# First DFT block turned by TensorE, columns taken in fours, and mod's shift row summed by TensorE, in an FNet and gMLP block

## The chip, the cores and the metric

The kernel runs on one core of a Trainium2 chip. A core has five engines, each with an instruction queue of its own that runs in order: TensorE (matrix products, PE in the profile, with its weight loads as PEld), VectorE (DVE), ScalarE (ACT), GpSimd (POOL) and SyncE (SP, which here only issues DMA transfers). The metric is the time on the device in microseconds, the median of several runs.

## What is computed

```python
mod = (_silu(c) @ w_mod).reshape(c.shape[0], 6, 1, -1)
sa, ca, ga, sb, cb, gb = (mod[:, 0], mod[:, 1], mod[:, 2], mod[:, 3], mod[:, 4], mod[:, 5])
h = _layernorm(x, axis=-1) * (1 + ca) + sa
x = x + ga * _A_ref(h, A_dft_seq_re, A_dft_seq_im, A_dft_hid_re, A_dft_hid_im)
h = _layernorm(x, axis=-1) * (1 + cb) + sb
x = x + gb * _B_ref(h, B_w_in, B_w_sp, B_b_sp, B_w_out)
```

`x` has 2048 rows of 512 floats. `_A_ref` is a Fourier mixing: h is multiplied by two 512 x 512 matrices along the columns and by two 2048 x 2048 matrices along the rows, `y = Cr a - Ci b` with `a = h Hr^T`, `b = h Hi^T`. `_B_ref` is a gated MLP: `z = gelu(h w_in)`, its second half is normed and multiplied by the 2048 x 2048 matrix `w_sp` along the rows, the result gates the first half, and `w_out` brings it back to 512 columns.

## The kernel before

**Products.** Each factor is split into a high part of reduced precision (fp32r) and the rest, its low part; a product a b is the sum of three (high high, high low, low high), issued by `matmul3` at L79, L80 and L81. The 2048 x 2048 matrices are read from memory in blocks of 512 x 512 and cut into chunks of 128 of their columns: a chunk n must stand with its column index on the partitions, that is transposed, and 512 row indices along the row.

**Main loop.** `src` lists the blocks: first those of Cr and Ci for the row quarter t = 0 (for each quarter g of the columns one of Cr, one of Ci), then t = 1 to 3, then h2 from memory, then w_sp. `load` brings block b into one of two buffers `stage`, as four transfers of 32 partitions (`load_block`, L131), in an order from which VectorE's transpose of 32 x 32 squares (`squares`, L142) makes chunk k. `prep_hi` (L153) makes T (transposed, by VectorE) and the high part ah (ScalarE, L165), `prep_lo` the low part al (VectorE, L174). `prep(n)` runs ahead: high part of chunk n + 3, low part of n + 2. `mm_a(n)` issues the twelve products of chunk n into four PSUM banks `gp`: four column groups k of h, three products each. Behind it `run(n)` issues what the table `fill` holds for this place (`at(n, f, ...)`), in the order in which it was entered. The order on each engine is the order in which the program issues (a manual schedule).

**Rows of x.** There are sixteen row tiles s of 128 rows. `load_x(g)` brings four; `stats_x` takes mean and variance (VectorE L87, L89), GpSimd makes the factor from them (L91, L92, L99), `norm_x` applies them on ScalarE (L103), `scale_x` multiplies by 1 + ca (L278), `shift_x` adds sa (L281). `hi_h` (ScalarE, L296) and `lo_h` (VectorE, L301) split the result into hh and hl. Tile 3 goes through `make_x` on VectorE (L287, L288). From tile 4 on, scaling and shift run on GpSimd. Chunk n of t = 0 multiplies tile s = 4 (n div 8) + n mod 4, so tiles 0 to 3 serve chunks 0 to 7, and tile 4 is first needed by chunk 8.

**mod.** The rows ca (number 1) and sa (number 0) are wanted at the start. Row 1 is summed by TensorE: four products of w_mod with a spread silu(c) (`scb`), in plain fp32 (L227). Of row 0, three quarters are summed by VectorE (L215, L220) and one by TensorE, which then spreads the sum over the partitions with a product by ones (L229). `keep_mod` copies the sum to SBUF (ScalarE, L209). `keep_busy` multiplies ones without use of the result (L236).

**Start.** SyncE issues x (tiles 0 to 2), w_mod for rows 1 and 0, block 0, x (tile 3), block 1 and x (tiles 4 to 7).

Of the kernel before, what the change touches and what calls it, by code (L numbers as in the profile page):

```python
# [8 lines left out]
F32 = mybir.dt.float32  # L9
# [4 lines left out]
P = 128  # L14
# [5 lines left out]
def fnet_gmlp_kernel(  # L20
# [115 lines left out]
    def load(b):  # L136
        if b < len(src):
            stage[b] = blocks.tile([P, 16, P], F32, tag="stage", bufs=2, name=f"stage{b}")
            load_block(stage[b], src[b])

    def squares(dst, block, k):
        nc.vector.transpose(dst.rearrange("p (b i) -> p b i", i=32), block[:, :, 32 * k:32 * k + 32])  # L142

    prepared = set()

    def prep(n):

        if n not in prepared:
            prepared.add(n)
            prep_hi(n + 3)  # L150
            prep_lo(n + 2)

    def prep_hi(n):  # L153
        if n >= NE:
            return
        b, k = divmod(n, 4)
        T[n] = blocks.tile([P, Q], F32, tag="t", bufs=2, name=f"t{n}")
        if N3 <= n < N4:

            nc.vector.transpose(T[n].rearrange("p (k a i) -> p a k i", k=4, i=32),  # L160
                                stage[b][:, :, 32 * k:32 * k + 32].rearrange("p (a k) i -> p a k i", k=4))
        else:
            squares(T[n], stage[b], k)
        AH[n] = blocks.tile([P, Q], F32R, tag="ah", bufs=4, name=f"ah{n}")
        nc.scalar.activation(AH[n], T[n], AF.Copy)  # L165
        if k == 3:
            stage.pop(b)
            load(b + 2)

    def prep_lo(n):  # L170
        if n >= NE:
            return
        AL[n] = blocks.tile([P, Q], F32R, tag="al", bufs=3, name=f"al{n}")
        nc.vector.tensor_tensor(AL[n], T.pop(n), AH[n].bitcast(F32), op=ALU.subtract)  # L174


    p2 = ctx.enter_context(ExitStack())
# [9 lines left out]
    nc.scalar.dma_start(ccol, c.rearrange("b (k p) -> p (b k)", p=P))  # L187
    ones = cpool.tile([P, P], F32, name="ones")
    nc.gpsimd.memset(ones, 1.0)
    mhalf = cpool.tile([P, 1], F32, name="mhalf")  # L190
    nc.gpsimd.memset(mhalf, -0.5)
    sc = cpool.tile([P, ND], F32, name="sc")
# [8 lines left out]
    def load_mod(j):  # L201
        wm[j] = [SP[-1].tile([P, D], F32, tag=f"wm{k}", bufs=2 if len(SP) == 1 else 1, name=f"wm{j}_{k}") for k in range(ND)]
        for k in range(ND):
            nc.sync.dma_start(wm[j][k], w_mod[k * P:(k + 1) * P, j * D:(j + 1) * D])

    def keep_mod(j, ps, pl, plus_one):
        if j not in mods:
            mods[j] = pl.tile([P, D], F32, name=f"mod{j}")
        nc.scalar.activation(mods[j], ps, AF.Copy, bias=1.0 if plus_one else 0.0)  # L209
# [12 lines left out]
    def sum_mod_first(j, k, pl, plus_one, summed=0):  # L222

        ps = bank(k, f"modp{j}")
        w = wm.pop(j)
        for m in range(summed, ND):
            nc.tensor.matmul(ps, scb[:, m, :], w[m], start=m == summed, stop=not summed and m == ND - 1)  # L227
        if summed:
            nc.tensor.matmul(ps, ones, w[0], start=False, stop=True)  # L229
        keep_mod(j, ps, pl, plus_one)  # L230

    def keep_busy(n, k):
# [26 lines left out]
    def load_x(g, ks=range(4)):  # L259

        if g not in XG:
            XG[g] = spool.tile([P, 4, D], F32, tag="x", bufs=2, name=f"x{g}")
        k0, k1 = ks[0], ks[-1] + 1
        v = x.rearrange("(g a k i) d -> g a i k d", g=NQ, a=4, i=32)
        for a in range(4):
            nc.sync.dma_start(XG[g][32 * a:32 * a + 32, k0:k1, :], v[g, a][:, k0:k1, :])
        for k in ks:
            X[4 * g + k] = XG[g][:, k, :]

    def stats_x(s):  # L270
        NRM[s] = norm([X[s]], "x")

    def norm_x(s):
        LN[s] = spool.tile([P, D], F32, tag="xn", bufs=4, name=f"xn{s}")
        apply(LN[s], X.pop(s), NRM.pop(s))

    def scale_x(s, eng=nc.vector):
        eng.tensor_tensor(LN[s], LN[s], mods[1], op=ALU.mult)  # L278
# [10 lines left out]

    def parts_h(s, t):  # L290

        return t[s].rearrange("p k (a i) -> p k a i", i=32), LN[s].rearrange("p (a k i) -> p k a i", a=4, i=32)

    def hi_h(s):
        h_hi[s] = hpool.tile([P, ND, P], F32R, name=f"hh{s}")
# [17 lines left out]
    def mm_a(n):  # L313
        t, r = divmod(n, 8 * NQ)
        j, s = ((r // 4) % 2, r // 8 * 4 + r % 4) if t == 0 else (r // NS, r % NS)
        if s == 0:
            for k in range(ND):
                GP[t, j, k] = bank(4 * j + k if t == 0 else ring[0] % 6, f"gp{t}_{j}_{k}")
                ring[0] += t > 0
        ah, al = AH.pop(n), AL.pop(n)  # L320
        for k in range(ND):
# [62 lines left out]
    def load_wi(e, k0):  # L384

        raw = wpool[0].tile([P, 2, FH], F32, tag="wraw", bufs=2, name=f"wraw{e}_{k0}")
        v = w_in.rearrange("(a k i) f -> a i k f", a=4, i=32)
        for a in range(4):
            nc.sync.dma_start(raw[32 * a:32 * a + 32], v[a][:, k0:k0 + 2, e * FH:(e + 1) * FH])
        for k in range(2):  # L390
            wraw[e, k0 + k] = raw[:, k, :]

# [139 lines left out]
            mm([n])  # L532


    load_x(0, range(3))
    load_mod(1)
    load_mod(0)
    load(0)
    load_x(0, range(3, 4))
    load(1)  # L540
    load_x(1)
    keep_busy(2, 5)
    for s in range(3):
        stats_x(s)
    for s in range(3):
        norm_x(s)
    sum_mod(0, range(3))
    sum_mod_first(1, 7, spool, True)
    sum_mod_first(0, 6, spool, False, 3)
    keep_busy(3, 5)  # L550
    for s in range(3):
        scale_x(s)
    shift_x(0, nc.vector)
    hi_h(0)
    shift_x(1, nc.vector)
    hi_h(1)
    lo_h(0)
    shift_x(2, nc.vector)
    lo_h(1)
    prep_hi(0)  # L560
    prep_lo(0)
    hi_h(2)
    prep_hi(1)
    prep_lo(1)
    lo_h(2)
    make_x(3)
    prep_hi(2)
    at(0, hi_h, 3)
    at(1, lo_h, 3)
    at(1, load_x, 2)  # L570
    at(9, load_x, 3)
# [200 lines left out]
```

## Time and profile before

| | |
|---|---|
| median of 3 runs | 1002.78 us (1002.72 to 1003.27) |
| the profiled execution's own time | 1003.15 us |
| its span, first to last instruction | 1001.4 us |
| granted TensorE clock, mean | 0.997 |
| instructions | 11608 |
| moved by DMA | 114.28 MB |

The profile is one execution, taken by the hardware profiler. Busy time says how long an engine worked, not what the end waited for; a wait is put down to what came last before the engine went on. In a group of instructions the text reads out<-in, with partitions x elements, then the count, the busy time in us and the mean in ns, then the idle time of the engine just before them. L numbers are lines of the kernel before.

### The profile page before, as it was taken

The page shows a single profiled execution, that of the slowest core. Times are in us where ns is not written, and L with a number is a line of the kernel's source. Part 1 is how long each engine was busy: PE and PEld are TensorE (multiplying, and loading weights), DVE is VectorE, ACT ScalarE, POOL GpSimd, SP SyncE. Part 2 cuts the span into 40 slices and gives each one's busy share as a digit, 9 for nine tenths or more (in the row PEclk, how much of TensorE's full clock was granted, in tenths as well). Part 3 has the DMA queues.
Part 4 walks back from the last instruction along what each step waited for, and adds up shares of the span by engine and source line. Part 5 has one row for each costly group of instructions (what it writes and reads, how often), then busy time and mean ns, then how long its engine had stood idle before and what let it go on. Part 6 is the DMA issues. An engine that isn't in the chain of part 4 may idle for free.

```text
span 1001.4 us, 11608 instructions
## 1 busy us (share of the span) xinstructions
PE 988.9 (99%) x4350; PEld 818.5 (82%) x4350; DVE 543.1 (54%) x820; ACT 295.9 (30%) x450; POOL 172.9 (17%) x281
## 2 busy tenths in 40 slices
PE   7999999999999999999999999999999999999998
PEld 3878888788888888888888998888888888888886
DVE  6888864876475546547433676565332622262315
ACT  3444531332232313222543665431111111111101
POOL 1576002022210122004321121102000200020001
PEclk8999999999999999999999999999999999999999
DMA  9786761565355343555553132435225222532141
GB/s 250 150 189 138 157 147 53 137 168 137 95 138 114 83 119 98 123 126 163 190 204 116 43 80 48 116 68 152 65 63 158 53 64 64 158 67 50 42 137 43
DMA packets 145961, 114.28 MB, mean 114 GB/s; under 512 B 7024, under 2 KB 125808, under 8 KB 145904
## 3 DMA queue, kind: packets, MB, share of 16 engines
q1 hardware_dynamic: 139296, 93.61, 39.6%
q0 software_dynamic: 6080, 19.93, 5.4%
q8 instruction: 34, 0.56, 0.2%
q14 instruction: 23, 0.19, 0.1%
q10 hardware_dynamic: 528, 0.00, 0.0%
HBM read 93.59 MB, written 19.92 MB: 113 GB/s over the span
## 4 chain that ended last, share of the span: by engine, by line
PE 94%; POOL 2%; issue 1%; DVE 1%; DMA 1%; ACT 0%; SPq 0%; DVEq 0%; POOLq 0%
PE gp L81 11%; PE gp L80 11%; PE gp L79 10%; PE gw L79 10%; PE gw L81 10%; PE gw L80 10%; PE yp L81 3%; PE yp L80 3%; PE yp L79 3%; PE z2p L80 3%; PE z2p L79 3%; PE z2p L81 3%; PE z1p L79 3%; PE z1p L80 3%; PE z1p L81 3%; PE op L81 2%
## 5 line engine op out<-in xcount | busy, mean ns | idle before, releaser
L174 DVE TENSOR_TENSOR al<-t,ah 128x512 fp32r<-128x512 f32 x224 | 161.6, 721 | 271.6 <-PE gw L80 142.6
L165 ACT ACTIVATE ah<-t 128x512 fp32r<-128x512 f32 x224 | 141.8, 633 | 541.8 <-PE gw L81 212.2
L79 PE MATMUL gp<-ah,hh 128*128 128x512 f32 x512 | 201.1, 393 | 3.1 <-ACT ah L165 2.7
L80 PE MATMUL gp<-al,hh 128*128 128x512 f32 x512 | 200.7, 392 | 0.6 <-DVE al L174 0.6
L81 PE MATMUL gp<-ah,hl 128*128 128x512 f32 x512 | 200.4, 391 | 0.0
L81 PE MATMUL gw<-ah,zl 128*128 128x512 f32 x448 | 174.3, 389 | 0.0
L80 PE MATMUL gw<-al,zh 128*128 128x512 f32 x448 | 174.3, 389 | 0.0
L79 PE MATMUL gw<-ah,zh 128*128 128x512 f32 x448 | 174.3, 389 | 0.0
L142 DVE STREAM_TRANSPOSE t<-stage 128x512 f32<-128x512 f32 x208 | 146.2, 703 | 4.6 <-DMA stage<-in_A_dft_seq_im_dram 1.7
L79 PEld LDWEIGHTS gp<-ah,hh 128*128 128x128 f32 x512 | 96.8, 189 | 24.7 <-ACT ah L165 3.5
L80 PEld LDWEIGHTS gp<-al,hh 128*128 128x128 f32 x512 | 96.8, 189 | 21.9 <-DVE al L174 1.7
L81 PEld LDWEIGHTS gp<-ah,hl 128*128 128x128 f32 x512 | 96.8, 189 | 20.5 <-DVE hl L301 0.5
L81 PEld LDWEIGHTS gw<-ah,zl 128*128 128x128 f32 x448 | 84.1, 188 | 17.6
L80 PEld LDWEIGHTS gw<-al,zh 128*128 128x128 f32 x448 | 84.1, 188 | 17.4
L79 PEld LDWEIGHTS gw<-ah,zh 128*128 128x128 f32 x448 | 84.1, 188 | 17.3
L496 POOL TENSOR_TENSOR u<-u,g 128x512 f32<-128x512 f32 x16 | 21.4, 1339 | 336.1 <-DVE g L494 336.1
L367 POOL DMA_DIRECT2D x_d<-xr x16 | 8.8, 551 | 246.3 <-DVE xr L366 246.3
L79 PE MATMUL yp<-hth,gh 128*128 128x512 f32 x128 | 49.8, 389 | 0.0
L80 PE MATMUL yp<-htl,gh 128*128 128x512 f32 x128 | 49.8, 389 | 0.0
L81 PE MATMUL yp<-hth,gl 128*128 128x512 f32 x128 | 49.8, 389 | 0.0
L80 PE MATMUL z2p<-wil,ah 128*128 128x448 f32 x128 | 46.7, 365 | 0.0
L79 PE MATMUL z2p<-wih,ah 128*128 128x448 f32 x128 | 46.7, 365 | 0.0
(106 smaller groups left out, 1165.4 us busy)
## 6 DMA issues: line engine op xcount, KB each, us to landing
stage<-in_A_dft_seq_re_dram SPq DMA_DIRECT2D x64, 256.0 KB, 4.8
stage<-in_A_dft_seq_im_dram SPq DMA_DIRECT2D x64, 256.0 KB, 5.0
stage<-in_B_w_sp_dram SPq DMA_DIRECT2D x64, 256.0 KB, 4.7
stage<-h_d SPq DMA_DIRECT2D x32, 256.0 KB, 4.6
z_d<-z POOLq DMA_DIRECT2D x28, 256.0 KB, 5.6
u<-z_d SPq DMA_DIRECT2D x4, 1792.0 KB, 8.2
wm<-in_w_mod_dram SPq DMA_DIRECT2D x24, 256.0 KB, 5.5
xr<-in_A_x_dram POOLq DMA_DIRECT2D x16, 256.0 KB, 3.2
```

What stands on the lines that cost most here:

```text
L79: nc.tensor.matmul(acc, ah, bh, start=first, stop=False)
L80: nc.tensor.matmul(acc, ah, bl, start=False, stop=False)
L81: nc.tensor.matmul(acc, al, bh, start=False, stop=last)
L142: nc.vector.transpose(dst.rearrange("p (b i) -> p b i", i=32), block[:, :, 32 * k:32 * k + 32])
L165: nc.scalar.activation(AH[n], T[n], AF.Copy)
L174: nc.vector.tensor_tensor(AL[n], T.pop(n), AH[n].bitcast(F32), op=ALU.subtract)
L367: nc.gpsimd.dma_start(x2_d[t][i * P:(i + 1) * P, :], x2)
L496: eng.tensor_tensor(U[t][:, f, :], U[t][:, f, :], g, op=ALU.mult)
```

## The change

It has four parts.

- **Block 0** is loaded as whole rows (`load_whole`: four transfers of 128 partitions) and turned by TensorE: `turn(k)` issues four transposes of 128 x 128 against an identity into a PSUM bank, from which the high and the low part of chunk k are taken. The high part of chunk 0 is made by VectorE. The identity is made on GpSimd at the start.
- **Columns in fours.** Chunk k of a block is no longer made of four runs of 32 columns but of every fourth column, k, k + 4, k + 8 and so on. VectorE's transposes read their source in steps of four floats. The rows of x are tiled alike: tile k of a quarter holds every fourth row, so a partition's four rows lie side by side in memory; h is read in steps of four floats when it is split (`parts_h`), and w_in is loaded likewise. For the four chunks a quarter of the second GELU half, the step lies in the reading of T (`like`).
- **x by tile**: one transfer for each `load_x` in place of four, and at the start one for tiles 0 and 1, one for tile 2, one for tile 3.
- **mod's row 0** is summed by TensorE alone. Tile 0 gets its shift straight from PSUM. The idle products behind it are gone. Tile 3 is normed on ScalarE like the others.

The first chunk's twelve products are issued in another order: four by ah, four by al, four with hl.

```diff
+    def load_whole():
+        stage[0] = blocks.tile([P, 16, P], F32, tag="stage", bufs=2, name="stage0")
+        v = stage[0].rearrange("p (q a) s -> p q (a s)", q=4)
+        for q in range(4):
+            nc.sync.dma_start(v[:, q, :], src[0][128 * q:128 * q + 128, :])
+
+    def turn(k):
+        T[k] = bank(4 + k, f"t{k}")
+        v = stage[0].rearrange("p (q a) (i k) -> p q k (a i)", q=4, k=4)
+        for q in range(4):
+            nc.tensor.transpose(T[k][:, 128 * q:128 * q + 128], v[:, q, k], ident)
+
     def squares(dst, block, k):
-        nc.vector.transpose(dst.rearrange("p (b i) -> p b i", i=32), block[:, :, 32 * k:32 * k + 32])
+        nc.vector.transpose(dst.rearrange("p (b i) -> p b i", i=32),
+                            block.rearrange("p b (i k) -> p k b i", k=4)[:, k])
...
+    def like(a, n):
+        return a.rearrange("p (k m) -> p k m", k=4) if N3 <= n < N4 else a
...
-        T[n] = blocks.tile([P, Q], F32, tag="t", bufs=2, name=f"t{n}")
-        if N3 <= n < N4:
-            nc.vector.transpose(T[n].rearrange("p (k a i) -> p a k i", k=4, i=32),
-                                stage[b][:, :, 32 * k:32 * k + 32].rearrange("p (a k) i -> p a k i", k=4))
-        else:
+        if n > 3:
+            T[n] = blocks.tile([P, Q], F32, tag="t", bufs=2, name=f"t{n}")
             squares(T[n], stage[b], k)
         AH[n] = blocks.tile([P, Q], F32R, tag="ah", bufs=4, name=f"ah{n}")
-        nc.scalar.activation(AH[n], T[n], AF.Copy)
+        if N3 <= n < N4:
+            T[n] = T[n].rearrange("p (m k) -> p k m", k=4)
+        if n == 0:
+            nc.vector.tensor_copy(AH[n], T[n])
+        else:
+            nc.scalar.activation(like(AH[n], n), T[n], AF.Copy)
...
+    ident = spool.tile([P, P], F32, name="ident")
+    make_identity(nc, ident)
...
-        v = x.rearrange("(g a k i) d -> g a i k d", g=NQ, a=4, i=32)
-        for a in range(4):
-            nc.sync.dma_start(XG[g][32 * a:32 * a + 32, k0:k1, :], v[g, a][:, k0:k1, :])
+        v = x.rearrange("(g p k) d -> g p k d", g=NQ, k=4)
+        nc.sync.dma_start(XG[g][:, k0:k1, :], v[g][:, k0:k1, :])
...
-        return t[s].rearrange("p k (a i) -> p k a i", i=32), LN[s].rearrange("p (a k i) -> p k a i", a=4, i=32)
+        return t[s], LN[s].rearrange("p (m k) -> p k m", k=4)
...
-    load_x(0, range(3))
+    load_x(0, (0, 1))
     load_mod(1)
+    load_x(0, (2,))
     load_mod(0)
-    load(0)
-    load_x(0, range(3, 4))
+    load_whole()
+    load_x(0, (3,))
     load(1)
     load_x(1)
     keep_busy(2, 5)
...
-    sum_mod(0, range(3))
     sum_mod_first(1, 7, spool, True)
-    sum_mod_first(0, 6, spool, False, 3)
-    keep_busy(3, 5)
...
+    ps = sum_mod_first(0, 6, spool, False)
+    turn(0)
+    turn(1)
+    nc.vector.tensor_tensor(LN[0], LN[0], ps, op=ALU.add)
     hi_h(0)
+    prep_hi(0)
+    prep_lo(0)
+    prep_hi(1)
+    lo_h(0)
     shift_x(1, nc.vector)
     hi_h(1)
+    prep_lo(1)
     lo_h(1)
...
+    prepared.add(0)
+    at(0, turn, 2)
+    at(0, turn, 3)
+    at(0, prep_hi, 2)
+    at(0, stats_x, 3)
+    at(0, norm_x, 3)
+    at(0, shift_x, 2, nc.vector)
+    at(0, hi_h, 2)
+    at(0, prep_lo, 2)
+    at(0, lo_h, 2)
+    at(0, prep_hi, 3)
+    at(0, scale_x, 3)
+    at(1, shift_x, 3, nc.vector)
+    at(1, hi_h, 3)
```

TensorE's queue at the start, before (modp is the sum of a row of mod, busyp the idle products, gp the sums of the main loop):

```order
L227 MATMUL modp1_194<-wm1_3_123,scb_108 128x512
L227 MATMUL modp0_201<-wm0_3_131,scb_108 128x512
L229 MATMUL modp0_201<-wm0_0_128,ones_102 128x512
L236 MATMUL busyp_206<-busy_109,ones_102 128x512 x3
L79 MATMUL gp0_0_0_265<-ah0_226,hh0_214 128x512
L80 MATMUL gp0_0_0_265<-al0_228,hh0_214 128x512
L81 MATMUL gp0_0_0_265<-ah0_226,hl0_219 128x512
```

and in the changed kernel, where t is a PSUM bank with a turned chunk:

```order
L249 MATMUL modp1_177<-wm1_3_125,scb_113 128x512
L249 MATMUL modp0_198<-wm0_0_131,scb_113 128x512
L249 MATMUL modp0_198<-wm0_1_132,scb_113 128x512
L249 MATMUL modp0_198<-wm0_2_133,scb_113 128x512
L249 MATMUL modp0_198<-wm0_3_134,scb_113 128x512
L153 MATMUL t0_205<-ident_104,stage0_139 128x128 x4
L153 MATMUL t1_210<-ident_104,stage0_139 128x128 x4
L345 MATMUL gp0_0_0_233<-ah0_218,hh0_216 128x512
```

Two products, a spread and three idle products ahead of the first product of the main loop became four products and eight transposes; eight more transposes (turn 2 and 3) follow behind chunk 0.

VectorE's queue from the last scaling to the first low part, before (xn are the row tiles, t the transposed chunks):

```order
L278 TENSOR_TENSOR xn2_189<-xn2_189,mod1_199 128x512
L281 TENSOR_TENSOR xn0_185<-xn0_185,mod0_204 128x512
L281 TENSOR_TENSOR xn1_187<-xn1_187,mod0_204 128x512
L301 TENSOR_TENSOR hl0_219<-xn0_185,hh0_214 128x512
L281 TENSOR_TENSOR xn2_189<-xn2_189,mod0_204 128x512
L301 TENSOR_TENSOR hl1_222<-xn1_187,hh1_217 128x512
L142 STREAM_TRANSPOSE t0_224<-stage0_136 128x512
L174 TENSOR_TENSOR al0_228<-t0_224,ah0_226 128x512
```

and in the changed kernel, from the last scaling to the low part of tile 1:

```order
L300 TENSOR_TENSOR xn2_194<-xn2_194,mod1_182 128x512
L586 TENSOR_TENSOR xn0_164<-xn0_164,modp0_198 128x512
L183 CAST ah0_218<-t0_205 128x512
L194 TENSOR_TENSOR al0_220<-t0_205,ah0_218 128x512
L323 TENSOR_TENSOR hl0_224<-xn0_164,hh0_216 128x512
L303 TENSOR_TENSOR xn1_175<-xn1_175,mod0_203 128x512
L194 TENSOR_TENSOR al1_229<-t1_210,ah1_222 128x512
L323 TENSOR_TENSOR hl1_231<-xn1_175,hh1_227 128x512
```

Between the last scaling and the first high part stand one addition and the cast; the shifts of tiles 1 and 2 and both hl moved behind it, and the transposes of chunks 0 to 3 left the queue.

More of the change, by code (lines that the diff above doesn't have):

```diff
@@ L173, in prep_lo @@
         AL[n] = blocks.tile([P, Q], F32R, tag="al", bufs=3, name=f"al{n}")
-        nc.vector.tensor_tensor(AL[n], T.pop(n), AH[n].bitcast(F32), op=ALU.subtract)
+        nc.vector.tensor_tensor(like(AL[n], n), T.pop(n), like(AH[n], n).bitcast(F32), op=ALU.subtract)
     p2 = ctx.enter_context(ExitStack())
@@ L230, in sum_mod_first @@
         keep_mod(j, ps, pl, plus_one)
+        return ps
     def keep_busy(n, k):
@@ L320, in mm_a @@
         ah, al = AH.pop(n), AL.pop(n)
+        if n == 0:
+            for k in range(ND):
+                nc.tensor.matmul(GP[t, j, k], h_hi[s][:, k, :], ah, start=True, stop=False)
+            for k in range(ND):
+                nc.tensor.matmul(GP[t, j, k], h_hi[s][:, k, :], al, start=False, stop=False)
+            for k in range(ND):
+                nc.tensor.matmul(GP[t, j, k], h_lo[s][:, k, :], ah, start=False, stop=False)
+            return
         for k in range(ND):
@@ L386, in load_wi @@
         raw = wpool[0].tile([P, 2, FH], F32, tag="wraw", bufs=2, name=f"wraw{e}_{k0}")
-        v = w_in.rearrange("(a k i) f -> a i k f", a=4, i=32)
-        for a in range(4):
-            nc.sync.dma_start(raw[32 * a:32 * a + 32], v[a][:, k0:k0 + 2, e * FH:(e + 1) * FH])
+        v = w_in.rearrange("(p k) f -> p k f", k=4)
+        nc.sync.dma_start(raw, v[:, k0:k0 + 2, e * FH:(e + 1) * FH])
         for k in range(2):
@@ L542, in fnet_gmlp_kernel @@
     keep_busy(2, 5)
[L543 to L546, printed above, removed]
-    sum_mod(0, range(3))
-    sum_mod_first(1, 7, spool, True)
-    sum_mod_first(0, 6, spool, False, 3)
-    keep_busy(3, 5)
-    for s in range(3):
-        scale_x(s)
-    shift_x(0, nc.vector)
+    stats_x(0)
+    norm_x(0)
+    stats_x(1)
+    norm_x(1)
+    sum_mod_first(1, 7, spool, True)
+    stats_x(2)
+    scale_x(0)
+    norm_x(2)
+    scale_x(1)
+    scale_x(2)
+    ps = sum_mod_first(0, 6, spool, False)
+    turn(0)
+    turn(1)
+    nc.vector.tensor_tensor(LN[0], LN[0], ps, op=ALU.add)
     hi_h(0)
+    prep_hi(0)
+    prep_lo(0)
+    prep_hi(1)
+    lo_h(0)
     shift_x(1, nc.vector)
     hi_h(1)
-    lo_h(0)
-    shift_x(2, nc.vector)
+    prep_lo(1)
     lo_h(1)
[L560 to L568, printed above, removed]
+    prepared.add(0)
[12 more added lines that the diff above has]
+    at(1, hi_h, 3)
     at(1, lo_h, 3)
```

## The prediction

> **What bounds the kernel now.** First the busy times and the slices of the page, then who keeps TensorE waiting, then the start step by step.
>
> ```profile
> PE 988.9 (99%) x4350; PEld 818.5 (82%) x4350; DVE 543.1 (54%) x820; ACT 295.9 (30%) x450; POOL 172.9 (17%) x281
> PE   7999999999999999999999999999999999999998
> DVE  6888864876475546547433676565332622262315
> ```
>
> TensorE is busy for 988.9 of 1001.4 us; only the first slice and the last are not full. A change that leaves the number of products alone can win at the start, or lose wherever VectorE, 0.8 busy over the first slices, stops keeping up. The waits of TensorE and the windows (the columns behind the engines are granted clock, DMA share, GB/s):
>
> ```profile
> PE gp L79 <- ACT ah L165: 2.7, 1, 2.7
> PE gp L79 <- ACT hh L296: 0.3, 1, 0.3
> 15.40:19.50 4.10, 1.38 (x5) 0.32 (x3) 3.31 (x7) 1.94 (x4) 0.00 (x0) 0.96 1.21 243
> 19.50:25.90 6.40, 6.40 (x14) 4.78 (x15) 5.19 (x9) 1.08 (x2) 1.05 (x2) 0.50 0.97 201
> 26.00:53.00 27.00, 26.91 (x119) 21.91 (x117) 23.65 (x37) 13.14 (x21) 17.02 (x21) 1.00 0.81 162
> 53.00:80.00 27.00, 26.72 (x116) 21.75 (x117) 22.66 (x36) 13.07 (x21) 20.58 (x26) 1.00 0.68 156
> 80.00:107.00 27.00, 27.00 (x119) 21.99 (x118) 23.19 (x37) 12.32 (x21) 13.34 (x17) 1.00 0.90 183
> 107.00:134.00 27.00, 27.00 (x121) 22.33 (x120) 23.33 (x37) 12.80 (x22) 0.00 (x0) 1.00 0.53 106
> ```
>
> Before the first product of the main loop TensorE stands for 2.7 us, and then runs 6.40 us at a granted clock of 0.50, which costs 3.2 us. The chain of waits gives the start in order:
>
> ```profile
> 2.10 4.01 DMA x<-in_A_x_dram
> 6.12 6.04 DMA wm<-in_w_mod_dram
> 12.21 1.12 PE modp L227 x2
> ...
> 14.22 0.61 ACT mod L209
> 14.86 0.70 DVE xn L281
> 15.58 0.64 ACT hh L296
> ...
> 18.14 0.63 DVE t L142
> 18.80 0.64 ACT ah L165
> ```
>
> The loads of w_mod end at 12.2, and from there one VectorE queue (three scalings, three shifts, two hl, the transpose) leads to the first product at 19.5. A second limit stands behind it, and no wait of TensorE names its length: the row tiles 4 to 7 are made on GpSimd, one after the other. Two rows of the timeline of VectorE (where it starts, and what two operations back to back take) and pieces of the chain of waits:
>
> ```profile
> 31.96 0.68 DVE L87 BATCH_NORM_STATS2 bstx<-x 128x6 f32<-128x512 f32 x1
> 14.86 1.29 DVE L281 TENSOR_TENSOR xn<-xn,mod 128x512 f32<-128x512 f32 x2 [0.36 <-ACT mod L209]
> ```
>
> ```profile
> 35.63 0.56 POOL rsx L92
> ...
> 36.55 1.79 POOL xn L278
> ...
> 48.96 0.83 ACT xn L103
> ...
> 51.24 1.31 POOL xn L281
> 52.58 0.64 ACT hh L296
> ```
>
> From the statistics of tile 4 (31.96) to the high part of tile 7 (53.2) it takes 21.25 us, nearly all of it GpSimd work, and TensorE waits 0.3 us for that tile at chunk 11: the two stand almost level now.
>
> **The change, part by part.**
>
> *mod's scale.* The issues on SyncE:
>
> ```profile
> 0.72 1.80 SPq L266 DMA_DIRECT2D x<-in_A_x_dram  x4
> 2.57 3.97 SPq L204 DMA_DIRECT2D wm<-in_w_mod_dram  x8
> 6.23 0.69 DVE L87 BATCH_NORM_STATS2 bstx<-x 128x6 f32<-128x512 f32 x1 [1.27 <-DMA x<-in_A_x_dram]
> 6.87 3.67 PE L227 MATMUL modp<-wm,scb 128*128 128x512 f32 x8 [1.59 <-DMA wm<-in_w_mod_dram]
> ```
>
> Four x transfers at 0.45 us stood ahead of w_mod; one does now, so w_mod comes 1.4 us earlier and its four products (eight passes at 0.43 us) start at 5.5 in place of 6.87 and end at 8.9. The statistics of x waited until 6.23 for the four pieces and run about a microsecond earlier. GpSimd makes the identity ahead of its first small operation; its queue is empty there, so I cost that at nothing.
>
> *mod's shift.* Three VectorE operations and two products become four products, 8 x 0.43 = 3.4 us, behind the scale's: 8.9 + 3.4 = 12.3. Their operands had landed at 12.2 with the block's short pieces mixed in; if they are no earlier, the end is 13.0. The scale is copied by 9.8 (0.6, behind the norm of tile 1) and the three scalings are done by 11.7, so the add for tile 0 runs from 12.4 to 13.1, and its high part is there at 13.8.
>
> *The first block turned by TensorE.* No row shows such a transpose. From below it costs a weight load, 0.19 us; from above two loads and two passes of 128 columns, 2 x (0.19 + 0.11) = 0.6 us:
>
> ```profile
> L227 PEld LDWEIGHTS modp<-wm,scb 128*128 128x128 f32 x10 | 1.7, 188 | 7.1 <-issue 4.0 <-DMA wm<-in_w_mod_dram 2.5 <-DVE mvx L89 0.6
> L142 DVE STREAM_TRANSPOSE t<-stage 128x512 f32<-128x512 f32 x208 | 146.2, 703 | 4.6 <-DMA stage<-in_A_dft_seq_im_dram 1.7
> L301 DVE TENSOR_TENSOR hl<-xn,hh 128x512 fp32r<-128x512 f32 x16 | 11.9, 746 | 8.1 <-ACT hh L296 7.8
> L496 DVE TENSOR_TENSOR u<-u,g 128x512 f32<-128x512 f32 x12 | 14.8, 1234 | 0.4
> L160 DVE STREAM_TRANSPOSE t<-stage 128x512 f32<-128x512 f32 x16 | 11.4, 710 | 0.3
> L301 DVE TENSOR_TENSOR hl<-xn,hh x16: 658/693/1105, 16.2 to 94.8; 128x512 fp32r<-128x512 f32 x16
> ```
>
> I take 0.25 us, near the load: turn(0) ends at 13.5 (12.9 to 14.9), the cast to the high part at 14.2, and the first product starts at **14.5** (13.9 to 15.6), 5.0 us earlier. The longest stand of TensorE before it is now under 1 us in place of 2.7, so the clock stays at 1.00 and chunk 0 takes 12 x 0.227 = 2.7 us (27.00 us for 119 products in the window from 80 to 107). turn(2) and turn(3) add 2.0 us of TensorE behind it, under which VectorE works.
>
> *VectorE up to tile 4.* Eighteen operations stand between the cast and the statistics of tile 4 (al 0 to 5, hl 0 to 3, the statistics and the scaling of tile 3, three shifts, transposes 4 to 6); back to back one takes 0.62 us (two shifts took 1.29). That is 14.2 + 11.2 = 25.4. Waits come on top: al 2 for turn(2), which is queued behind chunk 0, 0.3; hl 2, because on ScalarE its high part stands behind the norm of tile 3, which waits for GpSimd's small operations on the statistics (some 1.3, the power alone 0.56; then norm 0.83 and high part 0.64, of which VectorE fills 1.4), 1.3; hl 3 for its high part, 0.7; some ten hand-overs at 0.06. The statistics of tile 4 start at **28.3 to 28.9**, 3.1 to 3.6 us earlier than 31.96.
>
> *GpSimd's chain caps it.* TensorE alone would be at chunk 11 by 28.3 + 7 x 2.72 = 47.3. The chain allows 28.7 + 21.25 = 49.95, against 53.2. So TensorE waits about 2.6 us there, and what is left is 3.2 us, although the first product comes 5 us earlier and the clock gives 3.2 more. Behind it the tiles come every second chunk and nothing else is shorter.
>
> *Every fourth column.* All 228 transposes that stay on VectorE, and the reads of xn for hh and hl, step over 16 bytes; the second GELU half moves the step to the reads of t. No row before reads a step like that. From below it costs nothing (an engine does not get faster by it), from above the slowest 512-element operation on VectorE, 1234 ns: 0 to 0.53 us each. The nearest rows of the same operation are those with other patterns, 703 and 710 ns, which do not tell patterns apart: I take **nothing**, and keep the other end as a rival. The single transfers for x and w_in in place of four each save SyncE time, of which nothing waits: nothing.
>
> Sum: 1003.15 us (the profiled execution's own time, 1.75 over its span) - 3.2 = 999.95; that execution stands 0.37 over the median 1002.78, so **999.7**.
>
> **The rivals.**
>
> *Stepped reads are slow (slower than before).* VectorE has spare 3.35, 4.34, 3.81 and 3.67 us in the four 27 us windows above, with 12, 10, 10 and 16 transposes:
>
> ```profile
> 26.00:53.00 27.00, 7.80 (x12) 1.00 0.81 162
> 53.00:80.00 27.00, 6.90 (x10) 1.00 0.68 156
> 80.00:107.00 27.00, 7.03 (x10) 1.00 0.90 183
> 107.00:134.00 27.00, 10.64 (x16) 1.00 0.53 106
> ```
>
> At 1.1 us each (the longest hl), 0.4 more, they exceed the spare by 1.4, 0, 0.2 and 2.7 us, and thirteen hl add 5.2: 9.5 - 3.2 = 6.3 slower, 1009. At 1234 ns: 3.0 + 1.0 + 1.5 + 4.8 + 6.9 = 17.2, less 3.2: 1017. It decides from about 0.95 us a transpose. For it: VectorE is the engine without spare just there. Against it: no row. [...]
>
> *The clock drops all the same (no change).* If the passes that turn do not hold the clock, TensorE counts as idle from 12.3 to 14.5, not far from the 2.7 us after which it fell to 0.50. 3.2 us are lost then, of which the 2.6 us before chunk 11 hide a part; with VectorE paced by TensorE I give back 2: 1001.7. [...]
>
> *GpSimd's chain starts no earlier (no change).* If only hl reads slowly (0.4 x 4 ahead of tile 4), or turning takes 0.6 us each, the statistics of tile 4 come 1.5 us earlier, not 3.2: 1001.4.
>
> **How the numbers follow.** About 0.2%, 2.0 us, is what a measurement of this kernel can tell from no change. Chances: forecast 0.42 (998.4 to 1000.8); the two cases without change 0.20 (1000.8 to 1004.5); stepped reads at some 1.1 us 0.17 (1005 to 1012); at 1.2 us and over 0.21 (1012 to 1022). Faster 0.43, same 0.19, slower 0.38. To leave out no more than 2 in 10 the range runs from 998.4 to 1014; the likeliest case's own is 998.4 to 1000.8.
>
> **What would show it.** First product at 14 to 15.6 with clock 1.00; turns at 0.2 to 0.6 us; statistics of tile 4 near 28.7; TensorE waiting 2 to 3 us for hh before chunk 11; the transposes still near 703 ns. The forecast is wrong if these take 1 us or more, if the window behind the first product has clock 0.50, or if chunk 11 waits for nothing.

## The result, and the profile after

| | before | after |
|---|---|---|
| median | 1003.02 us (1002.72 to 1003.33, 4 runs) | 1019.89 us (1019.18 to 1020.73, 4 runs) |
| ratio | | 1.0166 (95% interval 1.0154 to 1.0178) |
| the profiled execution, its span | 1003.15 us, 1001.4 us | 1020.59 us, 1018.7 us |

The change makes the kernel 1.7% slower. The page of the changed kernel, busy times and slices:

```profile
PE 996.7 (98%) x4364; PEld 820.2 (81%) x4364; DVE 626.9 (62%) x814; ACT 308.3 (30%) x450; POOL 180.6 (18%) x284
PE   8888999999999999999999999999999999999998
```

VectorE works 84 us more with six instructions fewer, and TensorE's first four slices, not one, are below nine tenths. The same windows as before (engines, then granted clock, DMA share, GB/s), the costliest waits of TensorE up to 200 us, and the groups whose durations changed:

```profile
26.00:53.00 27.00, 23.08 (x90) 16.92 (x89) 21.19 (x29) 12.53 (x16) 13.06 (x16) 0.94 0.45 106
53.00:80.00 27.00, 23.39 (x99) 18.10 (x99) 21.68 (x30) 12.85 (x18) 18.63 (x24) 1.00 0.61 157
80.00:107.00 27.00, 24.09 (x99) 19.18 (x98) 21.49 (x29) 13.35 (x18) 18.89 (x22) 0.94 0.41 90
```

```profile
PE gp L79 <- ACT hh L318: 8.3, 5, 2.6
PE gp L81 <- DVE hl L323: 2.1, 6, 0.4
```

```profile
L156 DVE STREAM_TRANSPOSE t<-stage 128x512 f32<-128x512 f32 x220 | 238.5, 1084 | 3.2
L318 ACT ACTIVATE hh<-xn 128x512 fp32r<-128x512 f32 x16 | 17.7, 1103 | 4.1 <-DVE xn L303 1.9 <-POOL xn L303 1.5 <-DVE xn L586 0.8
L323 DVE TENSOR_TENSOR hl<-xn,hh 128x512 fp32r<-128x512 f32 x16 | 17.3, 1080 | 17.3 <-ACT hh L318 17.3
```

The transposes went from 703 to 1084 ns, hl from 746 to 1080, hh on ScalarE from 628 to 1103. In these three windows TensorE does 288 products where it did 354. It waits for hh, and VectorE itself stands 17.3 us for hh (7.8 before). Behind some of these stands the passes run slowly for a while, every 0.43 us in place of 0.23 (granted clock 0.94 over two of the windows): so it is behind the stands that end at 28.08 us (1.60 us long) and 87.10 (2.52), but not behind the longest, which ends at 61.85 (2.62).

The start, in the timeline of the changed kernel (start, duration):

```profile
6.22 0.21 ACT L215 ACTIVATE sc<-ccol 128x4 f32<-128x4 f32 x1 [3.74 <-DMA ccol<-in_c_dram]
7.02 10.10 PE L249 MATMUL modp<-wm,scb 128*128 128x512 f32 x16 [1.74 <-DVE scb L220]
16.96 1.12 PE L153 MATMUL t<-ident,stage 128*128 128x128 f32 x8
17.16 0.60 ACT L231 ACTIVATE mod<-modp 128x512 f32<-128x512 f32 x1 [2.14 <-PE modp L249]
17.79 0.69 DVE L586 TENSOR_TENSOR xn<-xn,modp 128x512 f32<-128x512 f32 x1 [1.54 <-ACT mod L231]
19.69 1.21 PE L345 MATMUL gp<-ah,hh 128*128 128x512 f32 x4 [1.61 <-ACT hh L318]
37.35 0.69 DVE L87 BATCH_NORM_STATS2 bstx<-x 128x6 f32<-128x512 f32 x1
```

The first product comes at 19.69 us (19.48 before), although the transpose of chunk 0, the shifts of tiles 1 and 2 and two hl no longer stand ahead of it. Eight turning passes take 1.12 us, 0.14 us each, less than the lower bound of the prediction. Everything ahead of them is late: silu(c) stands at 6.22 (3.76 before), mod's sixteen passes take 10.1 us, the addition waits for the copy of the same bank. Tile 4's statistics come at 37.35, before at 31.96.

From tile 8 on the changed kernel falls into a period: hh begins at 67.02, 73.33, 79.64, 85.96, every **6.31 us** per row tile (then at 92.94 and 99.25, with one step of 6.98). A row tile serves two chunks, for which TensorE needs 2 x 2.72 = 5.44 us. One such period:

```profile
68.14 1.09 DVE L323 TENSOR_TENSOR hl<-xn,hh 128x512 fp32r<-128x512 f32 x1 [1.20 <-ACT hh L318]
69.13 1.09 DVE L156 STREAM_TRANSPOSE t<-stage 128x512 f32<-128x512 f32 x1
70.15 0.73 DVE L194 TENSOR_TENSOR al<-t,ah 128x512 fp32r<-128x512 f32 x1
70.81 0.68 DVE L87 BATCH_NORM_STATS2 bstx<-x 128x6 f32<-128x512 f32 x1
71.62 1.06 DVE L156 STREAM_TRANSPOSE t<-stage 128x512 f32<-128x512 f32 x1
72.80 0.63 ACT L185 ACTIVATE ah<-t 128x512 fp32r<-128x512 f32 x1 [1.83 <-DVE t L156]
73.33 1.09 ACT L318 ACTIVATE hh<-xn 128x512 fp32r<-128x512 f32 x1
74.46 1.08 DVE L323 TENSOR_TENSOR hl<-xn,hh 128x512 fp32r<-128x512 f32 x1 [1.20 <-ACT hh L318]
```

It is a ring over two engines. VectorE does hl, a transpose, al, the statistics and a second transpose; ScalarE makes ah from that transpose, and hh stands behind ah in its queue; VectorE's next operation is hl, which needs that hh. Start to start the pieces are 0.99 + 1.02 + 0.66 + 0.81 + 1.18 + 0.53 + 1.13 = 6.32 us. Four of them read in steps of 16 bytes.

### The profile page after: what moved, and what is told of

It is laid out like the page before. It is cut to its first block, busy times and chain, and to the rows that moved or that the text cites. A ratio compares the mean times of both kernels' runs of the same rounds, so it can differ in the third digit from the quotient of the medians.

```text
span 1018.7 us, 11583 instructions
## 1 busy us (share of the span) xinstructions
PE 996.7 (98%) x4364; PEld 820.2 (81%) x4364; DVE 626.9 (62%) x814; ACT 308.3 (30%) x450; POOL 180.6 (18%) x284
## 4 chain that ended last, share of the span: by engine, by line
PE 88%; DVE 4%; issue 2%; ACT 2%; DMA 2%; POOL 1%; SPq 1%; ACTq 0%; DVEq 0%; POOLq 0%
PE gw L81 10%; PE gw L80 10%; PE gw L79 10%; PE gp L81 9%; PE gp L80 9%; PE gp L79 9%; PE yp L81 3%; PE yp L79 3%; PE yp L80 3%; PE z2p L79 3%; PE z2p L80 3%; PE z2p L81 3%; PE z1p L79 2%; PE z1p L80 2%; PE z1p L81 2%; PE op L80 2%
## 5 line engine op out<-in xcount | busy, mean ns | idle before, releaser
L185 ACT ACTIVATE ah<-t 128x512 fp32r<-128x512 f32 x223 | 149.2, 669 | 556.0 <-PE gw L81 209.8
L156 DVE STREAM_TRANSPOSE t<-stage 128x512 f32<-128x512 f32 x220 | 238.5, 1084 | 3.2
```

Source lines behind the costliest of these rows:

```text
L185: nc.scalar.activation(like(AH[n], n), T[n], AF.Copy)
```

## The experiments

Ratios are to the kernel before, in runs on the same chip.

**1. steps_alone: the kernel before, with only the columns in fours.**

```diff
-        nc.vector.transpose(dst.rearrange("p (b i) -> p b i", i=32), block[:, :, 32 * k:32 * k + 32])
+        nc.vector.transpose(dst.rearrange("p (b i) -> p b i", i=32),
+                            block.rearrange("p b (i k) -> p k b i", k=4)[:, k])
...
-        return t[s].rearrange("p k (a i) -> p k a i", i=32), LN[s].rearrange("p (a k i) -> p k a i", a=4, i=32)
+        return t[s], LN[s].rearrange("p (m k) -> p k m", k=4)
```

> The kernel before with only the columns taken in fours (transposes on VectorE, the split of h, the rows of x, w_in, the reads of T in the second GELU half); the start, the loads' order, mod and the first block as before. Theory S (the stepped reads are the whole loss, because VectorE and ScalarE run out of spare in the first 134 us): 1017 to 1022 us, the transposes at 1.08 us, TensorE with about 20 products fewer in each of the windows 26-53, 53-80 and 80-107. Theory R (the loss is in the new start: the turn, the late silu(c), the clock): 1003 to 1007 us.

Measured: 1019.77 us, ratio 1.0167 (1.0152 to 1.0182), the changed kernel's time, as theory S has it (the three windows have 16, 22 and 10 products fewer than before). The stepped layout, with the one transfer for each load of x and w_in that it allows, costs 16.9 us alone; on top of it all other parts of the change together give nothing.

**2. hybrid: the change, with the step only where the turned block needs it.** Chunks that meet the first 512 rows of x keep the fours, all else reads runs of 32 (and loads w_in and the later tiles of x as before).

```diff
+        part = block.rearrange("p b (i k) -> p k b i", k=4)[:, k] if step else block[:, :, 32 * k:32 * k + 32]
...
+            squares(T[n], stage[b], k, 4 * b < N2 and (b // 2 if b < 8 else b) % 4 == 0)
```

> The changed kernel, but only the blocks of Cr and Ci that meet the first 512 rows of x keep the columns in fours (block 0 is turned by TensorE as in the change, four transposes of block 1 are stepped at the start, eight in each later quarter); all other blocks, the split of h and w_in read in runs of 32 again. Theory S: the loss goes, 999 to 1004 us, transposes in runs at 0.70 us, hh at 0.63 us. Theory R: 1015 to 1020 us, as the changed kernel.

Measured: 1004.67 us, ratio 1.0019 (1.0009 to 1.0028): just outside the range that theory S gave, and not the 1015 of theory R. The step was the loss; but with all but 28 stepped transposes gone the new start does not win 3.2 us either. Its timeline (first product, statistics of tile 4, first product of chunk 11), its waits for hh (total, times, longest) and a window:

```profile
17.97 1.17 PE L351 MATMUL gp<-ah,hh 128*128 128x512 f32 x4 [1.15 <-ACT hh L324]
33.01 0.68 DVE L87 BATCH_NORM_STATS2 bstx<-x 128x6 f32<-128x512 f32 x1
54.24 0.50 PE L79 MATMUL gp<-ah,hh 128*128 128x512 f32 x1 [1.67 <-ACT hh L324]
```

```profile
PE gp L79 <- ACT hh L324: 2.8, 3, 1.7
53.00:80.00 27.00, 25.74 (x105) 20.82 (x106) 22.10 (x33) 12.43 (x20) 20.52 (x26) 0.94 0.70 160
```

The first product is 1.5 us earlier than before and at full clock, but tile 4's statistics are 1.0 us later. Three transposes of block 1 stand ahead of these statistics and are still stepped, which is 1.1 us. From there to tile 7's high part it takes 21.2 us, and TensorE waits 1.67 us for it ahead of chunk 11; from 56.1 to 59.1 us its passes then run at 0.43 us each. So a loss of the clock that the new start avoids at chunk 0 comes back here. This profiled execution took 1006.46 us, 1.8 over hybrid's median (1003.07 to 1006.58); whether the quicker ones are spared these slow passes, no trace shows.

**3. hl_runs and 4. h_steps: the split of h alone.** In hl_runs the changed kernel's hh and hl read runs of 32 again, the transposes stay stepped; h_steps steps only hh and hl, in the kernel before. In each the eight transposes of the 512 x 512 matrices go with the split.

```diff
-        return t[s], LN[s].rearrange("p (m k) -> p k m", k=4)
+        return t[s].rearrange("p k (a i) -> p k a i", i=32), LN[s].rearrange("p (a k i) -> p k a i", a=4, i=32)
```

> The changed kernel with only the split of h (hh on ScalarE, hl on VectorE) read in runs of 32 again; all transposes of the DFT blocks, h2 and w_sp stay stepped. Theory T (VectorE's throughput: the 24 or so transposes in the first 107 us are the larger part): 16 hl save 0.35 us each and the time falls by 3 to 6 us, 1013 to 1017. Theory H (the 0.48 us that each hh takes longer on ScalarE stands in front of TensorE at every row tile): falls by 10 us or more, below 1010.

> The kernel before with only the split of h (hh on ScalarE, hl on VectorE) and the eight transposes of the 512 x 512 matrices stepped; the transposes of the chunks read in runs. The counterpart of hl_runs, in which the time fell by 12 us. Theory G (a ring: per row tile VectorE makes two transposes, two low parts and hl, and stands while ScalarE makes ah and hh; it costs only what it lasts over the 5.44 us that TensorE needs for two chunks: 6.31 us with all stepped, 5.52 in hl_runs): the ring lasts 6.31 - 2 x 0.38 = 5.55 us, a row tile every 5.5 us from tile 8 on, and the time is 1004.5 to 1008. Theory H (the split of h as such costs 12 of the 17 us, since hh stands directly ahead of TensorE): 1013 to 1016.

Measured: hl_runs 1007.90 us, ratio 1.0045 (1.0030 to 1.0060); h_steps 1010.17 us, ratio 1.0072 (1.0058 to 1.0086). Taking the 32 operations on h out of the stepping gives back 12 us, as theory H for hl_runs has it; putting them in alone costs 7.2 (with the start of before): the parts do not add, as a ring wants it that costs only what it lasts over TensorE's 5.44 us. In hl_runs hh follows every 5.52 us (59.52, 65.06, 70.58), which looks like the ring less 0.33 for hl and 0.48 for hh. But the ring is open there: VectorE stands for hh only 0.3 us in all from 58 to 90 us and is nearly full, since one of the two al of a tile takes 1.36 us. By an estimate it falls beside GpSimd's shift: the norm ends at 61.94 us, and scaling and shift take 1.49 and 1.40 on the mean. The window of hl_runs, and two of its operations:

```profile
53.00:80.00 27.00, 25.29 (x109) 20.21 (x110) 26.08 (x36) 13.56 (x20) 20.67 (x25) 1.00 0.64 161
64.22 1.36 DVE L194 TENSOR_TENSOR al<-t,ah 128x512 fp32r<-128x512 f32 x1
65.73 0.71 DVE L323 TENSOR_TENSOR hl<-xn,hh 128x512 fp32r<-128x512 f32 x1
```

Neither theory had h_steps right: 5.55 us a tile was expected, and it is 5.94. Pieces of its timeline:

```profile
74.55 1.09 ACT L296 ACTIVATE hh<-xn 128x512 fp32r<-128x512 f32 x1
76.43 1.44 POOL L278 TENSOR_TENSOR xn<-xn,mod 128x512 f32<-128x512 f32 x1 [1.18 <-ACT xn L103]
77.29 1.13 DVE L174 TENSOR_TENSOR al<-t,ah 128x512 fp32r<-128x512 f32 x1
79.76 0.65 DVE L174 TENSOR_TENSOR al<-t,ah 128x512 fp32r<-128x512 f32 x1
80.49 1.09 ACT L296 ACTIVATE hh<-xn 128x512 fp32r<-128x512 f32 x1
```

With the transposes shorter, the first al now begins deep inside GpSimd's scaling of the next tile, and takes 1.13 us in place of 0.73; that takes 0.4 us of the saving away, the difference from 5.55 to 5.94. The slow al ends 0.55 us behind the scaling (77.87 us); the other al, beside small operations of GpSimd only, takes 0.65. The two coincide in time; by what GpSimd's work would slow it no run shows.

**5. hl_later: the ring opened by order.** All reads stay stepped; hl is entered one chunk behind hh (from tile 4 on, without 7 and 11).

```diff
-        at(n + 3, split_h, s)
...
+            at(n + 3, hi_h, s)
+            at(n + 4, lo_h, s)
```

> The changed kernel with all reads stepped, but hl of the row tiles from 4 on (without 7 and 11) entered one chunk later than hh, so that VectorE doesn't stand for hh. Theory G (it is the ring's length, 1.2 us of which are VectorE's stand ahead of hl): the row tiles from 8 on follow at 5.4 to 5.6 us in place of 6.31, VectorE's waits for hh fall from some 16 us to under 6, and the time to 1008 to 1013. Rival W (VectorE's and ScalarE's longer work as such, whatever the order): 1017 or more.

Measured: 1014.44 us, ratio 1.0117 (1.0103 to 1.0130): 5.4 us won by order alone, so the work as such (rival W) is not the whole; but the forecast was missed by 1.4 us: from tile 8 on a row tile follows every 5.85 us on the mean, not 5.4 to 5.6. VectorE's group of hl in this kernel, and TensorE's wait for it:

```profile
L323 DVE TENSOR_TENSOR hl<-xn,hh 128x512 fp32r<-128x512 f32 x16 | 22.0, 1377 | 6.4 <-ACT hh L318 6.4
PE gp L81 <- DVE hl L323: 6.2, 9, 2.5
```

VectorE's stand for hh fell from 17.3 to 6.4 us, but hl itself went from 1080 to 1377 ns, now that it falls beside GpSimd's scaling and shift (the hl at 67.49 us took 1.47, with GpSimd in the two from 66.81 to 70.07); and TensorE now waits 6.2 us for hl (2.1 in the changed kernel).

**6. probe: the disputed cost by itself.** Behind the output of the kernel before, rows of six equal operations that nothing needs:

```diff
+    one(lambda: V.transpose(ob, big[:, :, 0:32]))
+    one(lambda: V.transpose(ob, two))
+    one(lambda: V.transpose(ob, four))
...
```

> The kernel before, and behind its last row rows of six equal operations on VectorE and on ScalarE that nothing of the output needs: transposes, differences and copies of 128x512 with the source in steps of 1, 2 and 4 floats, in runs of 4 floats at a step of 16, with the destination in steps of 4 and of 128, and from PSUM in steps of 4. Theory P (what costs is each 16-byte hop of the source, whatever the operation): step 1 at 0.62 to 0.70 us, step 4 at 1.05 to 1.1 us on both engines, runs of 4 floats near step 1, PSUM with no extra cost. Rival (cost grows with the span that is read, so step 2 costs half of the extra), then step 2 at about 0.85 us and runs of 4 as slow as step 4. The time of the whole is that of the kernel before and some 60 to 90 us.

Measured, in one run of 1086.31 us (groups of the probe; the steps are named in the text):

```profile
L760 DVE STREAM_TRANSPOSE o<-big 128x512 f32<-128x512 f32 x6 | 4.2, 702 | 0.2
L761 DVE STREAM_TRANSPOSE o<-big 128x512 f32<-128x512 f32 x6 | 4.3, 712 | 0.2
L762 DVE STREAM_TRANSPOSE o<-big 128x512 f32<-128x512 f32 x6 | 6.6, 1092 | 0.2
L764 DVE TENSOR_TENSOR o<-big,sm 128x512 f32<-128x512 f32 x6 | 4.1, 688 | 0.2
L766 DVE TENSOR_TENSOR o<-big,sm 128x512 f32<-128x512 f32 x6 | 6.3, 1058 | 0.2
L767 DVE TENSOR_TENSOR o<-big,sm 128x512 f32<-128x512 f32 x6 | 4.2, 692 | 0.2
L768 DVE TENSOR_TENSOR d<-sm 128x512 f32<-128x512 f32 x6 | 6.4, 1066 | 0.2
L769 DVE COPY o<-big 128x512 f32<-128x512 f32 x6 | 2.6, 426 | 0.2
L770 DVE COPY o<-big 128x512 f32<-128x512 f32 x6 | 3.7, 619 | 0.2
L771 ACT ACTIVATE r<-big 128x512 fp32r<-128x512 f32 x6 | 3.8, 630 | 11.4 <-DVE big L748 11.2
L772 ACT ACTIVATE r<-big 128x512 fp32r<-128x512 f32 x6 | 4.0, 664 | 0.2
L773 ACT ACTIVATE r<-big 128x512 fp32r<-128x512 f32 x6 | 6.7, 1120 | 0.2
L774 ACT ACTIVATE r<-big 128x512 fp32r<-128x512 f32 x6 | 3.8, 630 | 0.2
L777 ACT ACTIVATE r<-pb 128x512 fp32r<-128x512 f32 x6 | 3.6, 597 | 0.2
```

Transposes in steps of 1, 2 and 4 floats take 702, 712 and 1092 ns; differences with one source in steps of 4 take 1058 in place of 688, ScalarE's copy 1120 in place of 630, with steps of 2 664. Runs of four floats at a step of 16 cost nothing (L767, 692 ns; L774, 630), and ScalarE's reading of PSUM in steps of 4 (L777, 597 ns) is no slower than its unstepped reading of SBUF (630); a difference that writes in steps of 4 takes 1066 ns (L768), as much as one that reads so. The span is the same for steps of 4 and for runs of four at a step of 16, so it is the hop of 16 bytes at every element that costs in these rows, not the span: theory P. Its price was not the same for every operation, though: VectorE's plain copy went from 426 only to 619 (L769, L770), 0.19 us more where the others pay 0.37 to 0.49.

**7. c_first.** In the changed kernel c's small load moves from ScalarE's queue to SyncE's, ahead of x.

```diff
-    nc.scalar.dma_start(ccol, c.rearrange("b (k p) -> p (b k)", p=P))
+    nc.sync.dma_start(ccol, c.rearrange("b (k p) -> p (b k)", p=P))
```

> The changed kernel with the small load of c issued by SyncE ahead of the first x transfer, in place of ScalarE's queue beside it. In the changed kernel silu(c) stood at 6.22 us, before at 3.76. Theory D (the small pieces of c lay behind the large x transfer in the DMA engines): silu(c) near 3.8, mod's products from about 5 us in place of 7.02, first product of the main loop 1.5 to 2.5 us earlier, and the whole 1 to 2.5 us faster (1017.5 to 1019). Rival (c is late for another reason, or the stepped VectorE queue eats what is won): silu(c) at 6 or the time within 0.5 us of 1019.9.

Measured: 1019.21 us, ratio 1.0161 (1.0144 to 1.0178), 0.7 less than the change, within the intervals and between what theory and rival gave; the first product of the main loop comes 1.0 us earlier.

```profile
3.00 0.20 ACT L215 ACTIVATE sc<-ccol 128x4 f32<-128x4 f32 x1 [1.00 <-DMA ccol<-in_c_dram]
6.86 9.23 PE L249 MATMUL modp<-wm,scb 128*128 128x512 f32 x16 [1.57 <-DVE mvx L89]
```

silu(c) is ready 3.2 us earlier, yet mod's products start at 6.86 in place of 7.02, as they did in the kernel before (6.87, for w_mod). Issued ahead of x c lands earlier, but a second limit stood right behind it. That it is w_mod is an inference: in the kernel before, where it was issued at 2.57 us, TensorE waited for it until 6.87; here it is issued at 1.76, the spread silu(c) is ready at 4.19, and the products start no earlier all the same. (The profile puts the wait down to VectorE's mvx, which the products don't read and which ends at about that time.)

**8. early4, 9. best, 10. best2, 11. best3: what the start is worth with most of the step gone.** Each adds to the one before, from hybrid on.

```diff
 early4
-    begin = [3, 4, 5, 7, 9, 11, 13, 15, 17, 19, 21, 22]
+    begin = [1, 2, 4, 6, 9, 11, 13, 15, 17, 19, 21, 22]
 best: c on SyncE as in c_first, and the copy of mod's shift row behind tile 0's addition and high part
     hi_h(0)
+    keep_mod(0, ps, spool, False)
 best2: behind chunk 0
+    at(0, shift_x, 2, nc.vector)
+    at(0, hi_h, 2)
     at(0, stats_x, 3)
     at(0, norm_x, 3)
...
+    at(0, scale_x, 3, nc.gpsimd)
+    at(1, shift_x, 3, nc.gpsimd)
 best3
-    keep_busy(2, 5)
+    keep_busy(3, 5)
```

> hybrid with the statistics of row tiles 4 to 7 entered behind chunks 1, 2, 4 and 6 in place of 3, 4, 5 and 7, and their norm, scaling, shift and split with them. Theory C (GpSimd's chain of 21 us from tile 4's statistics to tile 7's high part, which starts at 33.0 us in hybrid and at 31.96 in the kernel before, takes the lead that the new start has won): statistics at 29.5 to 30.5 us, TensorE's wait of 1.67 us ahead of chunk 11 gone, 1001.0 to 1003.0 us. Rival V (VectorE is full there: the statistics only push the transposes of chunks 5 to 8 back, and TensorE waits for these): 1004 us or more.

> early4 with the load of c on SyncE ahead of x, and tile 0's shift and high part entered ahead of the copy of mod's shift row, so that the addition no longer waits for that copy. Theory C and D: the first product of the main loop at 16.0 to 16.7 us in place of 17.97, all VectorE work behind it as much earlier, 999.5 to 1001.5 us. Rival (the transfers set the start: w_mod lands near 6.9 us either way, and block 1 and tiles 4 to 7 of x land after 25 us): within 0.5 us of early4.

> best with the start's order behind chunk 0 changed: tile 2's shift and high part ahead of tile 3's statistics and norm, and tile 3's scaling and shift on GpSimd, which is idle until tile 4. Theory Q (in best it is VectorE's and ScalarE's queue behind chunk 0 that holds chunks 2 and 3 back, 0.3 and 0.9 us of waits, and with them tile 4's statistics at 28.6): hh of tile 2 near 21.5 us in place of 23.1, tile 3's near 26 in place of 27.3, tile 4's statistics near 26 to 27, and the time 1000 to 1001.5. Rival (x of tiles 4 to 7 lands after 26 us, or GpSimd at tile 3 delays its own chain): tile 4's high part no earlier than 36.6, within 0.5 us of best's 1002.8.

> best2 with three idle products at the start in place of two, so that TensorE runs on until w_mod is there. In the changed kernel and all its variants the first passes of mod's products followed every 0.85 us until 9.7 to 12.3 us, in the kernel before every 0.43 us from the start. Theory K (TensorE's stand of 1.5 to 1.7 us ahead of these products leaves it at half the clock): every pass 0.43 us, mod's sixteen passes end near 13.8 in place of 15.3 us, the first product of the main loop about 1 us earlier, the time 0.5 to 1.3 us under best2's 1001.1. Rival (the last rows of w_mod or the first block land later than that, or the queue behind chunk 0 takes it): the time within 0.5 us of 1001.1.

Measured: early4 1003.91 us, ratio 1.0005 (0.9995 to 1.0014), between the two theories; best 1002.83, 0.9994 (0.9984 to 1.0004), a miss too, between theory and rival; best2 **1001.11**, 0.9982 (0.9973 to 0.9991), inside the range of theory Q; best3 **1000.74**, 0.9972 (0.9961 to 0.9983), within the 0.5 us of the rival. In early4 tile 4's statistics come at 29.54 and the wait ahead of chunk 11 is gone, but chunks 2 and 3 still wait for their hh (0.30 and 0.84 us) behind norms and shifts; best moves everything an us ahead and keeps those waits. In best2 the wait for tile 2's hh is gone (hh at 21.25 in place of 23.14), but tile 3's (26.79 in place of 27.29) still holds TensorE for 0.78 us, and tile 4's statistics come at 28.06, not at 26 to 27: theory Q had the time, but only one of its three signs, and the intervals of best and best2 overlap. Of best3, mod's sixteen passes and the first product of the main loop:

```profile
6.78 7.15 PE L250 MATMUL modp<-wm,scb 128*128 128x512 f32 x16
15.77 1.16 PE L352 MATMUL gp<-ah,hh 128*128 128x512 f32 x4 [0.40 <-DVE ah L184]
```

With TensorE kept at work until mod's products the passes take 7.15 us in place of 8.87 in best2, and the first product comes 1.5 us earlier, as theory K says, in one execution of each; against best2 the time moves by 0.4 us, inside the intervals, so that its worth is not settled.

**12. before_early: the order of the tiles alone.** The kernel before with early4's line.

> The kernel before with only the statistics of row tiles 4 to 7 entered behind chunks 1, 2, 4 and 6 in place of 3, 4, 5 and 7 (norm, scaling, shift and split with them). It tells how much of best2's gain the order of the tiles alone makes. Theory C (before, GpSimd's chain and TensorE stand level at chunk 11 with 0.3 us of wait, so an earlier chain alone gains at most that): 1002.4 to 1003.3 us. Rival (the order alone makes the gain): 1000.5 to 1002.

Measured: 1002.45 us, ratio 0.9991 (0.9981 to 1.0000): as theory C has it. So the order of the tiles alone hardly explains best3's gain (the intervals overlap only from 0.9981 to 0.9983); for best2 that isn't settled. Its first products of mod:

```profile
7.10 6.26 PE L227 MATMUL modp<-wm,scb 128*128 128x512 f32 x10 [1.82 <-DMA wm<-in_w_mod_dram]
```

Here ten passes take 6.26 us. In the quoted profile of the kernel before the first eight took 3.67, though nothing differs up to there: the quick passes at that place were that execution's, not the kernel's. TensorE stood 1.82 us ahead of them here and 1.59 there; the granted clock reads 1.00 in both.

One row goes with the time in all these kernels: the start of hh of the last row tile, 15, in the profiled execution.

| kernel | hh of tile 15, us | median, us |
|---|---|---|
| before | 94.11 | 1003.02 |
| changed | 109.01 | 1019.89 |
| steps_alone | 109.14 | 1019.77 |
| c_first | 108.18 | 1019.21 |
| hl_later | 103.50 | 1014.44 |
| h_steps | 101.45 | 1010.17 |
| hl_runs | 97.21 | 1007.90 |
| hybrid | 96.31 | 1004.67 |
| early4 | 94.01 | 1003.91 |
| before_early | 93.14 | 1002.45 |
| best | 93.02 | 1002.83 |
| best2 | 92.42 | 1001.11 |
| best3 | 90.91 | 1000.74 |

From that row to the median it is 908.4 to 911.0 us in all of them, so what was lost or won until then stays, to within 2.7 us. Of the changed kernel's 14.9 us here, 5.3 stand at tile 4 (45.22 against 39.94), 2.8 come between tile 4 and 7, and 5.8 of the remaining 6.8 from tile 8 to 13, at 6.45 us a tile against 5.29.

## Why the prediction was wrong

*Every fourth column taken as nothing.* This is the step that failed, and it holds all of the loss: 16.9 us in steps_alone, of which all but 1.8 us go in hybrid. The prediction had no row of such a read and took the lower end from rows whose patterns both read runs of 32 floats; these could not tell it apart. The measured price is 0.38 us a transpose, 0.33 a difference and 0.48 a copy on ScalarE, inside its bounds of 0 to 0.53.

*The rival on that side* had the right cause and the right duration (1.1 us), but 1009 for it. It counted VectorE's idle time as spare and left ScalarE's hh out. Idle VectorE was standing for hh, 1.2 us a tile in the ring, and could take no work: from tile 8 on the ring of 6.31 us against 5.44 is what counts, not the sum of busy times. Up to tile 7, where 8.1 of the 14.9 us are lost, the runs show that the step is the cause (hybrid is 7.2 us earlier at that tile), but what holds up that stretch is not taken apart here. The measured time lies in the band 1012 to 1022, which the prediction kept for transposes of 1.2 us and more; they took 1.08, so that the time lies there speaks for no mechanism of the prediction.

*mod's scale from 5.5, products at 0.43 us a pass.* Wrong in both terms. The products start at 7.02 (6.86 with c early), since what sets it is the arrival of c (silu(c) at 6.22) and, by the inference from c_first, of w_mod, not SyncE's issue; and the passes run at half that rate at first, at 10.1 us for sixteen in place of 6.8. The 0.43 us came from an execution in which they happened to run quickly.

*The addition for tile 0 straight from the bank.* It waited 0.6 us for the copy of the same bank by ScalarE, which the prediction left out; best, where the copy is entered behind it, has it right after the last product.

*Turning by TensorE.* Mis-sized on the safe side: 0.14 us a pass, not 0.25. In hybrid the granted clock is 1.00 from 13 to 53 us, through both pairs of turns, so the drop that the second rival feared did not come. Whether TensorE counts as busy while it turns, on which that rival's 1001.7 rests, no run shows: from mod's last pass to the first product it is 2.1 us there, turns included, and in the changed kernel the passes were slow behind stands of 1.60 and 2.52 us but not behind one of 2.62.

*VectorE's queue, and GpSimd's cap.* Right in length, the queue with some luck: from the addition to tile 4's statistics 15.9 to 16.5 us were forecast (12.4 to 28.3 or 28.9), and hybrid has 16.47 (16.54 to 33.01), but 1.1 us of that are the three stepped transposes, which the forecast put at nothing. The chain of 21.25 us has 21.2. Both only start 4.1 us later than forecast: 1.6 by the products' start, 2.0 by their passes, 0.6 by the copy. That eats the whole gain of 3.2 us. The third rival had foreseen that GpSimd's chain might start too late, for other reasons, and gave 1001.4 for a start 1.5 us earlier; in hybrid it starts 1.05 us later than before, at 1004.67.

*The sum.* 999.95 less 0.37 is 999.6, not 999.7; nothing hangs on it.

*Identity, single transfers.* The identity costs nothing that a wait shows. The single transfer is not free of effect: with it c landed 5.5 us after its issue, before 3.0.

## What to carry to other kernels

The layout that spared transfers at the start was paid here at the later reads of it (0.38 us a transpose, 0.33 a difference, 0.48 a copy on ScalarE): before a pattern goes into a loop, time one operation with that pattern; the rows of other patterns (703 and 710 ns) said nothing of its 1084. Where two engines hand work to each other in a fixed order, add up the ring from start to start and hold it against the period of the engine that bounds the kernel (6.31 us against 5.44 here); VectorE's idle time inside this ring, 1.2 us a tile, was no spare. And the start that was issued earlier was not earlier here: c landed 5.5 us after its issue in place of 3.0, mod's passes took 10.1 us, and the copy that read the same bank held the addition for 0.6.

## What was not expected of the hardware

- Reads of SBUF in steps of 2 floats cost at most 5.4% and in steps of 4 over 50%, in the probe's rows of VectorE's transposes and differences (702, 712, 1092 ns; 688 and 1058) and in ScalarE's copies (630, 664, 1120); VectorE's plain copy pays 45% (426, 619). Reading PSUM in steps of 4 takes ScalarE 597 ns.
- A load of 2 KB in small pieces, issued at the same moment as one of 512 KB, landed after 5.5 us; issued ahead of it, silu(c) stood at 3.00 us.
- An al of VectorE that began 0.58 us before the end of GpSimd's scaling took 1.13 us (h_steps), one that began 0.19 us before it 0.73 (changed kernel), one beside GpSimd's small operations alone 0.65; hl, moved beside scaling and shift in hl_later, took 1377 ns on the mean in place of 1080.
- How long TensorE stood did not decide alone whether its next passes were slow: in the changed kernel they were behind stands of 1.60 and 2.52 us, and not behind one of 2.62 us.
